# A list scheduler in the source for the S4D half of a two-layer kernel, and x's statistics moved to ScalarE

## The chip, the cores and the metric

One core of a Trainium2 chip runs the whole program. The engines are TensorE (PE in the profile; its weight loads PEld), VectorE (DVE), ScalarE (ACT), GpSimd (POOL) and SyncE (SP), which here only issues DMAs. The metric is the device time of one execution in microseconds (us), median of several runs. Each engine works through its own queue in order; waits between engines go through semaphores.

## The reference

The input x is 2048 x 640, one batch. Everything is float32.

```python
mod = (_silu(c) @ w_mod).reshape(c.shape[0], 6, 1, -1)
sa, ca, ga, sb, cb, gb = (mod[:, 0], mod[:, 1], mod[:, 2], mod[:, 3], mod[:, 4], mod[:, 5])
h = _layernorm(x, axis=-1) * (1 + ca) + sa
x = x + ga * _A_ref(h, ...)
h = _layernorm(x, axis=-1) * (1 + cb) + sb
x = x + gb * _B_ref(h, B_w1, B_w3, B_w2)
```

_A_ref is an S4D convolution along the 2048 positions: for each of the 640 channels the filter is K[l] = 2 Re sum over n of C[n] exp(A[n] dt l), with 128 complex modes n, and y = irfft(rfft(h, 4096) rfft(K, 4096)) + h D_skip. _B_ref is a gated FFN, (silu(h w1) * (h w3)) w2, with 1728 hidden units.

## The kernel before

The convolution is done by hand-written Fourier stages on TensorE, in five blocks of 128 channels (NB = 5). A block needs these pieces, named by the tiles that the profile shows:

- **Filter generation**, eight chunks of 16 channels (gen_chunk). POOL adds phases from two small tables (p to ph) and multiplies magnitudes from two tables of exponentials e (to yy and xx); ScalarE takes two sines and an absolute value per chunk (sn, ph, cs); DVE multiplies (five instructions, to yy and xx); TensorE forms 64 small products (kps), and ScalarE copies two chunks at a time out (ks). The tables p come from five integer shifts on DVE (tile step) and additions on POOL; the tables e from 24 small exponentials of al on ScalarE (param_exp).
- **h**, four pieces of 512 positions: x's columns are loaded again (xq), two rounds of four scalar_tensor_tensor on DVE apply the layer norm and the modulation rows rw (h_make, to xq and hb), a DMA stores hb to DRAM (hs), and one fetch brings the block's h back in another layout (xb).
- **The first stage**, 8 items from xb and 8 from ks, all into PSUM tiles ps, evicted to sp.
- **The spectra**, 8 steps: fh (from h) is copied to hz by ScalarE, two fk (from the filter) are multiplied with hz on DVE (fp), fz is the inverse step on TensorE, evicted to zt and stored to DRAM (zd).

The parameters of block 0 are worked out at the very start (param_part, some 30 DVE instructions over 128x128), those of blocks 1 to 4 together in batch (L798, the same over 128x512, tiles e and scratch). The start-up (early, L807) also loads x once in full (xs) for the layer norm's statistics (bn_stats on DVE, h_st), and w_mod, whose first half gives the rows rw (pm, prow) and whose second half gives the columns cols by three mod_col. The table wb of the spectra uses the memory that parts of w_mod and log_A held, so its load comes after them.

The order: every instruction up to the last spectra goes through the wrappers InOrder (L80 to 90), which chain each engine's instructions in the order of the source; that is why nearly all of them have line L88 in the profile, and groups are told apart by tile. After the start-up comes block 0's first stage, then batch, then the spectra of block 0 with the generation and the h of block 1 merged in by hand-set fractions of the TensorE work (merge L934, beside L947), then for each block its first stage and spectra with the next block's generation and h, and last the fifth block with the first two FFN weight splits (wh, wl) and some inverse rows (iy). Three PSUM banks (tag f) serve ps, fh, fk and fz.

After that the scheduling framework orders the rest: the remaining inverse rows (iy), the second layer norm and transposes (tp, ln2), and the FFN (gu, acc), in four blocks of 512 positions.

Of the kernel before, what the change touches and what calls it, by code (L numbers as in the profile page):

```python
# [10 lines left out]
F32 = mybir.dt.float32  # L11
# [18 lines left out]
EXPS = [(0, 0, i, 64 * i) for i in range(1, 8)] + [(1, 0, k, 512 * k) for k in range(1, 4)] + \  # L30
       [(0, 1, i, i) for i in range(1, 8)] + [(1, 1, k, 32 + 8 * k) for k in range(4)] + [(1, 2, k, 8 * k) for k in range(1, 4)]
# [66 lines left out]

class K:
# [34 lines left out]
    def rsqrt(self, pool, mv, n, tag):  # L134

        nc = self.nc
        v = pool.tile([P, n], F32, name=f"rs_v_{tag}", tag="rs_v")
        yi = pool.tile([P, n], I32, name=f"rs_y_{tag}", tag="rs_y")
        t = pool.tile([P, n], F32, name=f"rs_t_{tag}", tag="rs_t")
        nb = pool.tile([P, n], F32, name=f"rs_n_{tag}", tag="rs_n")  # L140
        nc.vector.tensor_scalar(v, mv[:, :, 1], EPS, None, op0=ALU.add)
        nc.vector.tensor_scalar(yi, v.bitcast(I32), 1, None, op0=ALU.logical_shift_right)
        nc.vector.tensor_scalar(yi, yi, -1.0, float(0x5F3759DF), op0=ALU.mult, op1=ALU.add)
        y = yi.bitcast(F32)
        for _ in range(3):
            nc.vector.tensor_mul(t, y, y)
            nc.vector.scalar_tensor_tensor(t, t, -0.5, v, op0=ALU.mult, op1=ALU.mult)
            nc.vector.scalar_tensor_tensor(y, t, 1.5, y, op0=ALU.add, op1=ALU.mult)
        self.last_rs = nc.vector.scalar_tensor_tensor(nb, mv[:, :, 0], -1.0, y, op0=ALU.mult, op1=ALU.mult)
        return y, nb  # L150
# [9 lines left out]
    def ln_end(self, pool, st, mv, tag):  # L160
        for j in range(4):
            self.nc.vector.bn_aggr(mv[:, j, :], st[:, j, :, :])
        return self.rsqrt(pool, mv, 4, tag)
# [17 lines left out]
    def mod_load_rows(self, k):  # L181
        self.nc.sync.dma_start(self.wm[k], self.w_mod[k * P:(k + 1) * P, :3 * D])

    def mod_row(self, pm, k):

        w = self.wm[k]
# [4 lines left out]

    def mod_rows(self, pm, ps):

        nc = self.nc
        m = self.ring("m")
        nc.gpsimd.memset(m[96:, 384:], 0.0)
        nc.scalar.activation(m[:, :384], pm[:, :384], AF.Copy)
        nc.scalar.activation(m[:96, 384:], pm[:96, 384:], AF.Copy)
        rows = self.rows
        for g in range(4):  # L200
            n = 512 if g < 3 else 384
            pr = ps.tile([P, 512], F32, name=f"prow{g}", tag="f", bufs=self.fb)
            nc.tensor.matmul(pr[:, :n], bc(self.ident[:, 32 * g], 1, P), m[:, :n], start=True, stop=True)
            for a in range(3):
                lo, hi = max(g * 512, a * D), min(g * 512 + n, a * D + D)
                if lo < hi:
                    nc.scalar.activation(rows[a][:, lo - a * D:hi - a * D], pr[:, lo - g * 512:hi - g * 512], AF.Copy)
        self.rA, self.rB = rows[1], rows[0]

    def mod_scale(self):  # L210
        nc = self.nc
        nc.vector.scalar_tensor_tensor(self.rA, self.rA, 1.0, self.rows[2], op0=ALU.add, op1=ALU.mult)
        nc.vector.tensor_mul(self.rB, self.rB, self.rows[2])

    def mod_load(self, a, w):
        self.nc.sync.dma_start(w, self.w_mod[:, (3 + a) * D:(4 + a) * D].rearrange("(k p) d -> p k d", p=P))

    def mod_col(self, ps, a, w):

        nc = self.nc  # L220
        m = self.ring(f"mc{a}")
        pm = ps.tile([P, 512], F32, name=f"pm{a}", tag="f", bufs=self.fb)
        for k in range(KT):
            for g in range(3):
                n = 256 if g < 2 else 128
                nc.tensor.matmul(pm[g * 32:(g + 1) * 32, :n], bc(self.sc[:, k], 1, 32), w[:, k, g * 256:g * 256 + n],
                                 start=(k == 0), stop=(k == KT - 1), tile_position=(0, g * 32))
        nc.scalar.activation(m[:96, :128], pm[:96, :128], AF.Copy)
        nc.scalar.activation(m[:64, 128:256], pm[:64, 128:256], AF.Copy)
        pv = pm[:, 256:262]  # L230
        nc.tensor.matmul(pv[:, 0:5:2], m[:96, :128], self.ident[:96, 0:96:32], start=True, stop=True)
        nc.tensor.matmul(pv[:, 1:4:2], m[:64, 128:256], self.ident[:64, 0:64:32], start=True, stop=True)
        add, mul = ((0.0, 1.0), (1.0, 1.0), (0.0, 0.5))[a]
        nc.vector.tensor_scalar(self.cols[:, a, :], pv[:, :KT], add, mul, op0=ALU.add, op1=ALU.mult)
# [10 lines left out]
    def h_stats(self, e, xs, b):  # L245
        nc = self.nc
        st = e.tile([P, 4, 2, 6], F32, name=f"h_st{b}", tag="h_st", bufs=2)
        for j in range(4):
            for h in range(2):
                nc.vector.bn_stats(st[:, j, h, :], xs[:, j, h * 320:(h + 1) * 320])  # L250
        for j in range(4):
            nc.vector.bn_aggr(self.h_mv[:, b * 4 + j, :], st[:, j, :, :])

    def h_scale(self):
        nm = self.gp.tile([P, NJ], F32, name="h_nm")
        self.nc.vector.tensor_scalar(nm, self.h_mv[:, :, 0], -1.0, None, op0=ALU.mult)
        self.h_rs = self.rsqrt(self.gp, self.h_mv, NJ, "h")[0], nm

    def h_load(self, pool, pc, b):
        t = pool.tile([P, 4, P], F32, name=f"xq{pc}{b}", tag="xq", bufs=2)  # L260
        self.x_slots(t, b, pc * P, pc * P + P)
        self.xq[pc, b] = t
# [85 lines left out]
    def param_alpha(self, ps, tag, bufs, bs):  # L348
        la = self.la[:, bs]
        n = la.shape[1]  # L350
        self.nc.vector.tensor_mul(la, la, bc(self.dts[0][:, bs], 2, P))
        pt = self.turn(ps, tag, bufs, la)
        self.nc.scalar.activation(self.al[:, bs], pt, AF.Copy)

    def param_exp(self, b, sl=slice(None)):

        E = self.E[b % 2]
        for t, m, i, k in EXPS[sl]:
            self.nc.scalar.activation(E[t][:, :, m, i], self.al[:, b], AF.Exp, scale=-float(k))

    def param_mag(self, b):
        V = self.nc.vector
        e2 = self.E[b % 2][1][:, :, 0]
        V.tensor_copy(e2[:, :, 0], self.mag[:, b])
        V.tensor_mul(e2[:, :, 1:4], e2[:, :, 1:4], bc(self.mag[:, b], 2, 3))

    def param_part(self, T, bs, mid=(None, None)):

        V, A = self.nc.vector, self.nc.scalar
        dtb, dt2b = (bc(x[:, bs], 2, P) for x in self.dts)  # L370
        cr, ci, ai, ar, aim, mx, m, k, at, s, fi = (T[x] for x in self.PARTS)


# [748 lines left out]
```

## Time and profile before

| | us |
|---|---|
| median of 3 runs | 1152.91 (1150.5 to 1154.26) |
| the profiled execution | 1157.82 |
| its span, first to last instruction | 1156.0 |
| TensorE busy | 983.8 (85% of the span) |
| TensorE weight loads busy | 800.1 (69%) |
| VectorE busy | 694.3 (60%) |
| ScalarE busy | 481.1 (42%) |
| GpSimd busy | 250.9 (22%), none of note after the last block's generation |
| mean granted TensorE clock | 0.934 |

The tables below the page's first part give busy time by stretches of the span. Rows of groups read: line, engine, operation, output<-inputs, shapes, count, then busy us and mean ns of one, then the idle time of the engine before them and what ended it. Rows of a timeline read: start, length, engine, line, operation, count, and in brackets the idle time before. A row of the chain of waits reads: start, length, what.

### The profile page before, as it was taken

How to read it: one execution, taken by the hardware profiler on the slowest of the kernel's cores; microseconds unless marked ns; L12 is line 12 of the kernel's file. 1: busy time of each engine (PE TensorE's matmuls, PEld its weight loads, DVE VectorE, ACT ScalarE, POOL GpSimd, SP SyncE). 2: the span in 40 equal slices, each digit the busy share in tenths (PEclk: the TensorE clock that was granted, in tenths of full speed). 3: DMA queues.
4: the chain of work that ended last, by engine and by line, in shares of the span. 5: the costliest groups of instructions: out<-in, count | busy, mean ns of one | idle time of the engine just before them, and what ended most of it. 6: DMA issues, size and time to landing. Idle time of an engine off the chain costs nothing.

```text
span 1156.0 us, 21214 instructions
## 1 busy us (share of the span) xinstructions
PE 983.8 (85%) x8663; PEld 800.1 (69%) x8663; DVE 694.3 (60%) x1263; ACT 481.1 (42%) x766; POOL 250.9 (22%) x226
## 2 busy tenths in 40 slices
PE   1445537887978979995999999999999999999996
PEld 0222526675876868974776888888888888888885
DVE  7872389879799697353676654545445454454432
ACT  5341445756657546431432433434334333333322
POOL 5750066565664746000000000000000000000000
PEclk9766867898998989997899999999999999999998
DMA  9829002322322413756874333523335333353311
GB/s 208 217 48 303 5 1 74 75 56 56 84 50 63 103 47 93 184 137 165 230 175 115 103 91 89 150 82 101 92 91 149 85 102 87 92 151 88 92 46 46
DMA packets 142978, 122.11 MB, mean 106 GB/s; under 512 B 14112, under 2 KB 125472, under 8 KB 141344
## 3 DMA queue, kind: packets, MB, share of 16 engines
q1 hardware_dynamic: 142880, 120.75, 39.8%
q8 instruction: 68, 1.11, 0.4%
q14 instruction: 30, 0.25, 0.1%
HBM read 99.75 MB, written 20.97 MB: 104 GB/s over the span
## 4 chain that ended last, share of the span: by engine, by line
PE 69%; DVE 14%; DMA 7%; ACT 4%; issue 3%; SPq 1%; POOL 1%; DVEq 0%; ACTq 0%
PE gu L738 11%; PE gu L739 11%; PE gu L740 11%; PE fz L88 6%; PE acc L773 5%; PE acc L774 5%; PE acc L775 5%; PE fk L88 4%; PE ps L88 3%; DVE yy L88 3%; DVE xq L88 2%; DVE hb L88 2%; PE kps L88 2%; DMA xs<-in_x 2%; PE fh L88 2%
## 5 line engine op out<-in xcount | busy, mean ns | idle before, releaser
L739 PE MATMUL gu<-xl,wh 128*128 128x512 f32 x540 | 212.3, 393 | 0.0
L738 PE MATMUL gu<-xh,wh 128*128 128x512 f32 x540 | 211.7, 393 | 0.5 <-ACT xh L668 0.5
L740 PE MATMUL gu<-xh,wl 128*128 128x512 f32 x540 | 211.4, 392 | 0.0
L88 PE MATMUL fz<-fp,wz 128*128 128x256 f32 x320 | 91.4, 429 | 46.3 <-DVE fp L88 46.0
L643 ACT ACTIVATE wh<-wr 128x640 fp32r<-128x640 f32 x105 | 71.9, 731 | 136.6 <-PE gu L739 131.3
L738 PEld LDWEIGHTS gu<-xh,wh 128*128 128x128 f32 x540 | 101.6, 188 | 25.5 <-issue 1.0
L739 PEld LDWEIGHTS gu<-xl,wh 128*128 128x128 f32 x540 | 101.8, 188 | 21.8
L740 PEld LDWEIGHTS gu<-xh,wl 128*128 128x128 f32 x540 | 101.6, 188 | 21.7
L88 POOL TENSOR_TENSOR yy<-e,e 128x512 f32<-128x512 f32 x80 | 87.4, 1113 | 114.4 <-PE kps L88 73.9
L88 PEld LDWEIGHTS fz<-fp,wz 128*128 128x128 f32 x320 | 63.4, 211 | 61.6 <-DVE fp L88 49.6
L773 PE MATMUL acc<-ah,w2h 128*128 128x512 f32 x260 | 103.8, 399 | 0.0
L774 PE MATMUL acc<-ah,w2l 128*128 128x512 f32 x260 | 102.2, 393 | 0.0
L706 POOL MEMSET w2l<- 64x640 f32 x3 | 1.9, 626 | 450.3 <-PE acc L774 450.3
L775 PE MATMUL acc<-al,w2h 128*128 128x512 f32 x260 | 96.4, 391 | 0.0
L753 DVE SCALAR_TENSOR_TENSOR a<-th,gu 128x512 f32<-128x512 f32 x52 | 35.7, 687 | 99.2 <-ACT th L752 99.0
L754 DVE TENSOR_TENSOR a<-a,gu 128x512 f32<-128x512 f32 x52 | 35.8, 688 | 97.2 <-PE gu L740 97.2
L88 PE MATMUL kps<-yy,xx 128*32 128x64 f32 x2560 | 56.8, 251 | 43.1 <-DVE xx L88 43.1
L88 PEld LDWEIGHTS kps<-yy,xx 128*32 128x32 f32 x2560 | 49.7, 127 | 62.3 <-issue 28.4
L644 DVE TENSOR_TENSOR wl<-wr,wh 128x640 fp32r<-128x640 f32 x105 | 82.2, 818 | 10.8 <-ACT wh L643 10.8
L752 ACT ACTIVATE th<-gu 128x512 f32<-128x512 f32 x52 | 31.1, 598 | 134.7 <-PE gu L740 134.7
L88 PE MATMUL fk<-sp,wb 128*64 128x128 f32 x1280 | 83.8, 281 | 1.9 <-ACT hz L88 1.9
L88 DVE TENSOR_TENSOR fp<-fk,hz 128x512 f32<-128x512 f32 x80 | 53.9, 686 | 47.7 <-PE fk L88 43.0
(190 smaller groups left out, 1711.6 us busy)
## 6 DMA issues: line engine op xcount, KB each, us to landing
wr<-in_w SPq DMA_DIRECT2D x104, 320.0 KB, 3.9
w2r<-in_w SPq DMA_DIRECT2D x52, 320.0 KB, 3.0
zd<-zt SPq DMA_DIRECT2D x40, 256.0 KB, 2.3
iz<-zd SPq DMA_DIRECT2D x24, 320.0 KB, 6.4
xs<-in_x SPq DMA_DIRECT2D x16, 320.0 KB, 14.9
xq<-in_x SPq DMA_DIRECT2D x80, 64.0 KB, 2.4
hs<-hb SPq DMA_DIRECT2D x20, 256.0 KB, 2.4
xb<-hs SPq DMA_DIRECT2D x20, 256.0 KB, 4.9
```

What stands on the lines that cost most here:

```text
L88: self.prev = self.k.order(f(*a, **kw), self.prev)
L643: self.nc.scalar.activation(H, v, AF.Copy)
L644: eng.tensor_tensor(Lo, v, H.bitcast(F32), op=ALU.subtract)
L738: nc.tensor.matmul(pg, wh[:, i, k, :], xh[:, k, :], start=(k == 0), stop=False)
L739: nc.tensor.matmul(pg, wh[:, i, k, :], xl[:, k, :], start=False, stop=False)
L740: nc.tensor.matmul(pg, wl[:, i, k, :], xh[:, k, :], start=False, stop=(k == KT - 1))
L752: nc.scalar.activation(th, gu[0], AF.Tanh, scale=0.5)
L753: nc.vector.scalar_tensor_tensor(a, th, 1.0, gu[0], op0=ALU.add, op1=ALU.mult)
L754: nc.vector.tensor_mul(a, a, gu[1])
L773: nc.tensor.matmul(acc[k], w2h[:, sl], ah, start=(m == 0), stop=False)
L774: nc.tensor.matmul(acc[k], w2l[:, sl], ah, start=False, stop=False)
L775: nc.tensor.matmul(acc[k], w2h[:, sl], al, start=False, stop=(m == 12))
```

## The change

A class Plan holds tasks: name, engine (or a choice of two), duration as written in the source, the tasks needed before, buffers taken and given back, a rank, whether it uses the port that POOL and DVE share, and bytes of DMAs. Its run method places the tasks one at a time, each on the engine where it can start first by these durations, the rank deciding among those that could start within 0.25 us, and calls the function that emits its instructions. So the order of the instructions on each engine still is fixed by the source, through the same wrappers; only what decides it is new. The functions batch, early, beside, merge, stages, gen_block, spectra and first_stage become task lists. Cut to its core:

```diff
-EXPS = [(0, 0, i, 64 * i) for i in range(1, 8)] + [(1, 0, k, 512 * k) for k in range(1, 4)] + \
-       [(0, 1, i, i) for i in range(1, 8)] + [(1, 1, k, 32 + 8 * k) for k in range(4)] + [(1, 2, k, 8 * k) for k in range(1, 4)]
+EXPS = ((0, 0, 0, 64.0), (0, 1, 0, 1.0), (1, 0, 0, 512.0), (1, 1, 4, 8.0), (1, 2, 0, 8.0))
...
+class Plan:
+    LAG = dict(PE=0.2, DVE=0.1, ACT=0.1, POOL=0.1, SP=0.0)
...
+                        if t[5] and s < port:
+                            s = port
...
+                m = min(c)[0]
+                x = min((y for y in c if y[0] <= m + near), key=lambda y: (y[1], y[0]))
...
+            if f:
+                f(e) if isinstance(eng, tuple) else f()
...
-    def h_stats(self, e, xs, b):
-                nc.vector.bn_stats(st[:, j, h, :], xs[:, j, h * 320:(h + 1) * 320])
-            nc.vector.bn_aggr(self.h_mv[:, b * 4 + j, :], st[:, j, :, :])
+        def sums(j):
+            nc.scalar.activation(xs[:, j], xs[:, j], AF.Copy, accum_out=self.h_nm[:, 4 * b + j:4 * b + j + 1])
+        def mean():
+            o = slice(4 * b, 4 * b + 4)
+            nc.vector.tensor_scalar(self.h_nm[:, o], self.h_nm[:, o], -1.0 / D, None, op0=ALU.mult)
+        def squares(j):
+            s = slice(4 * b + j, 4 * b + j + 1)
+            nc.scalar.activation(xs[:, j], xs[:, j], AF.Square, bias=self.h_nm[:, s], accum_out=self.h_ss[:, s])
...
+    def h_norm(self, pc, b):
+        for j in range(4):
+            s = slice(4 * b + j, 4 * b + j + 1)
+            self.nc.scalar.activation(x[:, j], x[:, j], AF.Identity, scale=rstd[:, s], bias=nb[:, s])
+    def h_mul(self, pc, b, eng):
+        eng.tensor_tensor(x, x, bc(self.rA[:, pc * P:pc * P + P], 1, 4), op=ALU.mult)
+    def h_add(self, pc, b, eng):
+        eng.tensor_tensor(hb, x.rearrange("p j (i a) -> p a j i", a=4),
+                          bc(self.rB[:, pc * P:pc * P + P].rearrange("p (i a) -> p a i", a=4), 2, 4), op=ALU.add)
...
-            for dst, src, k in ((p1[:, :, :, 0], by_t(pB), 0), (st[:, 0], pS, 1), (st[:, 1], pS, 2),
-                                (p2[:, :, :, 1], by_t(pS), 3), (p2[:, :, :, 2], by_t(pS), 4)):
-                self.last_step = V.tensor_scalar(dst, src, k, None, op0=ALU.logical_shift_left)
+        return [(.45, lambda: add(st[:, 0], pS, pS)),
+                (.45, lambda: add(st[:, 1], st[:, 0], st[:, 0])),
+                (.45, lambda: G.tensor_copy(p1[:, :, :, 0], by_t(pB))),
...
+    def exp_tasks(self, b):
+            self.eng(e).tensor_tensor(x[0], bc(self.al[:, b], 2, 8), bc(self.j8, 1, P), op=ALU.mult)
+        def exps():
+            for t, m, k, s in EXPS:
+                n = 8 if t == 0 else 4
+                A.activation(E[t][:, :, m, :], x[0][:, :, k:k + n], AF.Exp, scale=-s)
+        add(f"mag{b}", ("POOL", "DVE"), (1.08, .68), lambda e: self.eng(e).tensor_tensor(E[1][:, :, 0], E[1][:, :, 0], bc(self.mag[:, b], 2, 4), op=ALU.mult),
+            [f"exp{b}", f"turn{min(b, 1)}"], t, port=True)
...
+    def pbank(self, name):
+        self.banks += 1
+        if self.banks % 3 == 2:
+            return self.psx.tile([P, 512], F32, name=name, tag="x")
+        return self.psg.tile([P, 512], F32, name=name, tag="f", bufs=2)
...
+            add(n + "f", "PE", .92, lambda i=i: of_h(i), first, t, take=[("bank", 1)])
+            add(n + "h", "ACT", .6, lambda i=i: hold(i), [n + "f"], t - q, take=[("hz", 2)], give=[("bank", n + "f")])
+            add(n + "z", "PE", 1.76, lambda i=i: inverse(i), [n + "x0", n + "x1"], t + W["late"], take=[("bank", 1)],
...
+        for k in range(KT):
+            add(f"c{k}", "SP", 0, lambda k=k: load_w(k), ["x3", "h0.3.l"] + ([f"c{k - 1}"] if k else []), W["col"] + k, dma=[983040], take=[("xs", 1)])
...
+        S = lambda b: 80.0 + 62 * b
```

Beside the order, these pieces of work differ:

- x's statistics: instead of 32 bn_stats and 16 bn_aggr on DVE, 32 passes over 128x640 on ScalarE (16 sums, 16 sums of squared deviations) and four small DVE instructions.
- h: instead of 8 DVE instructions over 128x128 per piece, 4 ScalarE instructions over 128x128 (h_norm) and a multiply and an addition over 128x512 on DVE or POOL (in block 0 on DVE).
- The tables p: POOL makes the shifted copies by additions, for all but the first table.
- The tables e: one product of al with 0 to 7 over 128x1024 (al8, on POOL or DVE) and five exponentials of 1024 or 512 elements on ScalarE, in place of 24 of 128; mag is one multiply in place of a copy and a multiply.
- w_mod's second half comes as five row pieces (c0 to c4) that share the buffers of xs, and one set of products gives all cols.
- The parameters of blocks 1 to 4 (some 29 instructions, seven of which may go to POOL by choice) are tasks with a rank early in the start-up; D_skip is added to ks in four pieces.
- fz and first-stage evictions may go to ScalarE or DVE.

On SP the new order in the start-up is: parameters of all blocks, x's first two pieces, w_mod's first half around x's third, the small tables, x's fourth, block 0's four xq, then c0, wb, c1, c2, the first store of h, c3, two stores, c4, the last store, and the fetch of xb.

1052 lines of the change are left out of this document (609 added, 443 removed).

## The prediction

> **What bounds the kernel now.** I read first the busy time of each engine by stage, cut where the work changes, then the chain that ended last, then the groups and the timeline of one stage. Columns of the first view: stretch in us, its length, busy time of TensorE, of its weight loads, of VectorE (DVE), ScalarE (ACT) and GpSimd (POOL) with counts, granted clock, DMA share, GB/s.
>
> ```profile
> 0.00:40.00 40.00, 12.61 (x161) 5.75 (x161) 33.06 (x104) 20.87 (x47) 25.18 (x34) 1.00 0.95 240
> ...
> 0.00:116.31 116.31, 45.21 (x673) 25.60 (x673) 75.62 (x204) 44.53 (x80) 52.85 (x56) 0.77 0.72 193
> 116.31:131.54 15.23, 15.20 (x257) 14.96 (x256) 0.17 (x1) 8.98 (x15) 0.00 (x0) 1.00 0.03 8
> 131.54:153.47 21.93, 4.76 (x22) 4.30 (x23) 19.83 (x32) 6.49 (x15) 2.00 (x2) 0.61 0.00 0
> 153.47:192.00 38.53, 18.48 (x269) 15.18 (x268) 32.68 (x47) 18.42 (x35) 30.35 (x28) 0.76 0.14 37
> 271.00:350.00 79.00, 67.46 (x1153) 58.16 (x1153) 66.40 (x111) 48.46 (x78) 47.50 (x40) 0.95 0.27 69
> 472.97:531.30 58.33, 58.20 (x656) 49.42 (x656) 23.10 (x46) 19.86 (x33) 0.63 (x1) 1.00 0.68 176
> 565.00:1156.00 591.00, 581.55 (x2634) 469.56 (x2632) 297.33 (x515) 205.72 (x317) 1.88 (x3) 0.99 0.39 103
> ```
>
> From 565 on TensorE is busy 581.55 of 591 us; the change doesn't touch that part. Before it lie 531.3 us in which TensorE is full only at the end (472.97 to 531.30, 58.20 of 58.33, the last block's first stage and spectra). The start-up takes 116 us, then 15 us of first stage, then 22 us in which DVE works out the parameters of blocks 1 to 4 (the "batch") while TensorE has 4.76 us of work, then a slow stretch, then periods of 79 us for each block. The chain of waits (start, length, what) gives the prices of TensorE's work at full clock and what the start-up waits for:
>
> ```profile
> 29.32 16.83 DMA xs<-in_x
> 101.20 14.06 DMA wb<-in_t_wb
> 300.92 1.10 PE kps L88 x61
> 472.97 15.31 PE ps L88 x254
> 503.79 1.87 PE iy L88 x8
> 510.59 1.87 PE iy L88 x8
> ```
>
> One block's first stage is 15.3 us. The last block's spectra are 58.33 - 15.31 - 2 x 1.87 = 39.3. A chunk's product kps is 1.10, eight are 8.8. So a block costs TensorE 15.3 + 39.3 + 8.8 = 63.4 us, and a period takes 79.0: 15.6 us are lost. Timeline rows show most of them (start, length, engine, what, idle before):
>
> ```profile
> 349.84 3.78 PE L88 MATMUL fz<-fp,wz 128*128 128x256 f32 x8 [6.89 <-DVE fp L88]
> ...
> 299.03 1.89 PE L88 MATMUL fz<-fp,wz 128*128 128x256 f32 x8
> ...
> 257.06 4.78 DVE L88 SCALAR_TENSOR_TENSOR xq<-xq,h_nm,rw 128x128 f32<-128x128 f32 x4
> 261.76 5.23 DVE L88 SCALAR_TENSOR_TENSOR hb<-xq,rs_y_h,rw 128x128 f32<-128x128 f32 x4
> ...
> 271.63 1.13 DVE L88 SCALAR_TENSOR_TENSOR xq<-xq,h_nm,rw 128x128 f32<-128x128 f32 x4
> 272.68 1.50 DVE L88 SCALAR_TENSOR_TENSOR hb<-xq,rs_y_h,rw 128x128 f32<-128x128 f32 x4
> ...
> 259.50 2.19 POOL L88 TENSOR_TENSOR yy<-e,e 128x512 f32<-128x512 f32 x2
> ...
> 279.79 1.95 POOL L88 TENSOR_TENSOR ph<-p,p 128x1024 int32<-128x1024 int32 x1
> 294.32 2.09 POOL L88 TENSOR_TENSOR yy<-e,e 128x512 f32<-128x512 f32 x2 [1.96 <-PE kps L88]
> ```
>
> At the block boundary TensorE waits 6.89 us for DVE's product fp, and the matmuls after the wait run at half pace (3.78 against 1.89 us). DVE was late because eight instructions of h (xq, hb) took 4.78 + 5.23 = 10.0 us while POOL was working, against 1.13 + 1.50 = 2.6 while it was not. POOL's own pair took 2.19 instead of 2.09.
>
> **The change, part by part.** The sum is made on the end of the last spectra: Ts (block 0's spectra start), plus four periods, plus the last spectra with their two iy (39.3 + 3.7 = 43.0). Afterwards the instruction order is the same as before (iy, tp, gu), and the weights of the first two FFN steps are still split beside the last spectra, so 531.3 to the end moves as it is. The numbers count instructions in the new order of each engine.
>
> *Ts: batch, statistics and loads.* The batch goes from 131.54-153.47 into the start-up, so it leaves a stretch where nothing covered it. bn_stats leave DVE; 32 ScalarE passes over 128x640 come in (sum, then squares). No row has a ScalarE pass with an accumulator; the nearest is a plain 128x640 pass.
>
> ```profile
> L643 ACT ACTIVATE wh<-wr 128x640 fp32r<-128x640 f32 x105 | 71.9, 731 | 136.6 <-PE gu L739 131.3
> L88 DVE BATCH_NORM_STATS2 h_st<-xs 128x6 f32<-128x320 f32 x32 | 12.9, 475 | 4.6 <-DMA wz<-in_t_wz 4.6
> L88 DVE SCALAR_TENSOR_TENSOR hb<-xq,rs_y_h,rw 128x128 f32<-128x128 f32 x16 | 6.1, 445 | 0.0
> L88 DVE SCALAR_TENSOR_TENSOR xq<-xq,h_nm,rw 128x128 f32<-128x128 f32 x16 | 4.5, 348 | 0.0
> ...
> L88 ACT ACTIVATE al<-ptp 128x128 f32<-128x128 f32 x1 | 0.3, 277 | 2.5 <-PE ptp L88 2.5
> L88 DVE TENSOR_TENSOR fp<-fk,hz 128x512 f32<-128x512 f32 x18 | 12.1, 685 | 6.1 <-PE fk L88 5.9
> ```
>
> ScalarE: 44.5 + 32 x 0.73 (23.4; between 23 and, at double, 47) + 16 normalisations x 0.28 (4.5) + eight of the first stage's evictions x 0.6 (4.8) = 77 us, below 100 even with its waits for x's loads, which now hold the sines queued behind them. DMA: 193 GB/s x 116.3 us = 22.4 MB, at the 240 GB/s of the first 40 us 93 us; the loads are the same, but the table wb no longer stands at the end (101.20, 14 us). On SP the store of the last h piece and the fetch of xb now stand behind the last piece of w_mod's second half, which waits until TensorE has read an earlier piece; while TensorE is that idle in the start-up (45.2 of 116.3) this stays inside DMA's 93. DVE: 75.6 - 12.9 (statistics) - 10.6 (xq, hb) + 19.8 (batch) + 8 x 0.69 (5.5, the h multiplies and adds, now 128x512) + some 2.6 small = 80 us. But some 33 of these (25 of the batch, eight of h) have their operands in SBUF and run beside POOL now. The rows give 0 (POOL idle) to (10.0 - 2.6) / 8 = 0.9 us more for each, so 0 to 30 us; I take 0.6 each, 20, since POOL will have few gaps there. DVE then is done near 100 and is what ends last; the last chunk's product, its eviction and two first-stage items add 4. **Ts = 104**, ends 96 (no such waits, DMA's 93 and the fetch) and 124 (all waits plus what they pass on to POOL).
>
> *A period.* POOL now does 47.5 + ten copies and additions of 128x128 that replace DVE's shifts (5.0) + al8 (2.0, as ph) + mag (1.1) + about four of the eight h multiplies and adds (4.4) = 60 us. These rows price them:
>
> ```profile
> L88 POOL TENSOR_TENSOR p<-p 128x128 int32<-128x128 int32 x2 | 1.0, 500 | 0.0
> L88 POOL TENSOR_TENSOR xx<-e,e 128x512 f32<-128x512 f32 x8 | 8.9, 1112 | 0.0
> L88 POOL TENSOR_TENSOR ph<-p,p 128x1024 int32<-128x1024 int32 x8 | 15.7, 1962 | 3.3 <-ACT cs L88 3.2
> ...
> L88 DVE SCALAR_TENSOR_TENSOR hb<-xq,rs_y_h,rw 128x128 f32<-128x128 f32 x16 | 9.9, 680 | 0.0
> L88 DVE SCALAR_TENSOR_TENSOR xq<-xq,h_nm,rw 128x128 f32<-128x128 f32 x16 | 8.8, 607 | 0.0
> ...
> L88 ACT ACTIVATE sn<-ph 128x1024 f32<-128x1024 int32 x8 | 8.2, 1027 | 6.0 <-DVE xx L88 6.0
> L88 ACT ACTIVATE e<-al 128x128 f32<-128x128 f32 x24 | 6.1, 438 | 0.0
> L88 ACT ACTIVATE hz<-fh 128x512 f32<-128x512 f32 x8 | 4.8, 595 | 5.6 <-PE fh L88 5.6
> ```
>
> DVE loses 18.7 (xq, hb of a period), gains some four h instructions (2.8, and 3.6 of waits), so 66.4 falls to about 54. ScalarE: 24 small exponentials (6.1) become two of 1024 and three of 512 elements (3.9, by sn and hz); 16 normalisations add 4.5: 48.5 becomes 51. So TensorE's 63.4 is the longest, POOL's 60 next. The boundary stall (6.9) and the matmuls at half pace behind it (some 2.5) go, because h of the next block is made during the spectra and its store and fetch are queued ahead of need on SP; its xq loads come behind zd stores there, with buffers for two, and are issued a third of a period early. Without both a period would be 79.0 - 9.4 = 69.6. Of the remaining 6.2 of short stalls I let 4 stand: **67.4**, ends 63.4 and 69.6. Two PSUM buffers and one instead of three in one pool are the same three, and cost nothing unless their order of release differs (0 to 1 us).
>
> Sum: 104 + 4 x 67.4 + 43.0 = 416.6 against 531.3: **-114.7**. The profiled execution took 1157.8 us (span 1156.0); it becomes 1043.1. The median of the runs is 1152.9, so 4.9 lower: **1038 us**. Own range: Ts 96 and 63.4 give 392.6, so 1014; Ts 110 and 69.6 give 431.4, so 1053.
>
> **The rivals.** *Period bound by POOL and the port it shares.* For it: POOL's 60 us against 63.4 leave 3.4, and each DVE operation on SBUF may hold POOL 0.1 (2.19 against 2.09) up to 0.69. Against: POOL makes the next block's phases ahead, so its work may spread over the whole period. The page "SBUF — State Buffer" of the Trainium skill, section "Who interferes with whom", says that a VectorE instruction with two SBUF inputs contends with a GpSimd one that reads SBUF, and that the second to issue blocks until the first has finished; the rows agree for DVE (0.9 us each) and show much less for POOL. By that rule POOL's 60 would grow by 0.69 for each of some five such DVE instructions, to 63.4, level with TensorE; by the rows to 60.5. The forecast needs neither. With periods between 72 and today's 79 the end is 435 to 463, the time 1057 to 1085; middle 1071.
>
> *The start-up doesn't shrink.* The batch in a POOL-laden stretch pays the full 30 us and delays the chunks, or ScalarE's waits for x hold the sines: Ts = 124, 20 later, 1058. For it: the 116 us before were full of waits, and one ScalarE queue now carries loads' waits; against: no engine's sum reaches 116.
>
> *Slower.* Each engine runs a fixed order made from durations that its author wrote down; an instruction that is late holds all that stand behind it on its engine, and they hold other engines. The stretch 153.47-192.00 shows such a knot: TensorE busy 18.48 of 38.53 with DVE 32.68 and POOL 30.35. It decides from periods of (531.3 - 104 - 43) / 4 = 96 us on, where TensorE's share falls under 66%; at 100 us the end is 547, +15.7, 1169. Against it: today's periods, also with fixed orders, have 85%.
>
> **How the numbers follow.** First forecast (1014 to 1053) 0.60, POOL-bound periods 0.20, long start-up 0.14, slower 0.05, and 0.01 for an end within 0.3%, which is what this measurement can tell from no change. So faster 0.94, same 0.01, slower 0.05. The range is 1010 to 1082: below the floor of 1014 by the spread of the runs, up to nearly the whole of the two milder rivals.
>
> **What would show it.** Right: the first fk and fz of block 0 near 104 instead of behind 170; no stretch with TensorE idle and DVE alone; fz of successive blocks 67 us apart; no 7 us wait for fp at a boundary; h's DVE instructions near 0.7 to 1.6 us; the last fz near 417; the same 625 us behind it. Wrong: POOL without gaps and kps waiting for it (first rival); sines behind x statistics, or batch operations of 1.5 us and more (second); TensorE under 70% in the periods (third). A different clock or length behind the last spectra would make the prediction wrong in a part that I take as unmoved.

## The result, and the profile after

| | before | after |
|---|---|---|
| median of 4 runs each, same chip, us | 1153.59 (1150.5 to 1156.32) | 1072.07 (1071.69 to 1072.32) |
| ratio after to before | | 0.9294, 95% interval 0.9269 to 0.9318 |
| profiled execution (span), us | 1157.82 (1156.0) | 1072.27 (1070.5) |
| block 0's spectra start (Ts), us | 152.4 | 127.3 (forecast 104) |
| mean of the four periods, us | 84.0 (79.0 from 271 to 350) | 68.6 (forecast 67.4) |
| last spectra and two iy, us | 43.0 | 44.8 (forecast 43.0) |
| behind them, us | 624.7 | 624.0 (forecast unmoved) |

Before, block 0's spectra begin at 152.4 and the last block's at 488.2, by TensorE's timeline:

```profile
152.37 1.53 PE L88 MATMUL fh<-sp,wb 128*128 128x128 f32 x8
...
158.94 1.02 PE L88 MATMUL fz<-fp,wz 128*128 128x256 f32 x4
...
488.21 1.18 PE L88 MATMUL fh<-sp,wb 128*128 128x128 f32 x8
```

The four periods between them take 335.8 us, 84.0 each in the mean. The kernel became 81.5 us faster by the medians, and 1038 was forecast, 34 us less than the 1072.07 measured. Of the 85.5 us by which the span is shorter, Ts gives 25.1 and the four periods 61.4; the last spectra take 1.8 more, the rest 0.7 less. The first view of the changed kernel is busy time by stage, with the columns of the prediction's first view: the start-up, the four periods, the last spectra, the rest.

```profile
0.00:127.27 127.27, 58.23 (x889) 38.72 (x889) 92.17 (x181) 90.66 (x160) 73.11 (x88) 0.83 0.66 177
127.27:401.74 274.47, 260.09 (x4611) 228.17 (x4609) 202.21 (x289) 203.97 (x293) 222.65 (x203) 0.99 0.36 92
401.74:446.50 44.76, 42.74 (x400) 34.07 (x400) 20.20 (x41) 12.57 (x21) 0.00 (x0) 1.00 0.51 133
446.50:1070.50 624.00, 600.32 (x2712) 485.08 (x2712) 312.09 (x553) 215.48 (x329) 4.45 (x5) 0.98 0.42 110
```

Four periods take 274.47, so 68.6 each, with TensorE busy 260.09 of it; here the change did nearly what was forecast. In the start-up no engine is busy for more than 92 of 127 us. The timeline of TensorE at its end (start, length, engine, line, operation, and in brackets the idle time before and its releaser):

```profile
114.39 1.96 PE L87 MATMUL kps<-yy,xx 128*32 128x64 f32 x64 [2.72 <-DVE xx L87]
116.28 9.28 PE L87 MATMUL ps<-wk,xb 128*64 128x128 f32 x128
125.38 1.96 PE L87 MATMUL ps<-wk,ks 128*64 128x128 f32 x32
127.27 1.18 PE L87 MATMUL fh<-sp,wb 128*128 128x128 f32 x8
```

The group of all fz (count, busy us, mean ns, then the idle time before them):

```profile
L87 PE MATMUL fz<-fp,wz 128*128 128x256 f32 x320 | 79.3, 391 | 1.0 <-DVE fp L87 1.0
```

The last chunk's kps comes at 114.4, then all eight items of h's first stage and the last two of the filter's, and the first fh 12.9 us behind it. And in the periods the wait for fp at a block boundary (6.89 us before) is gone: all 320 fz together were waited for 1.0 us.

What came first in the start-up is in the timelines of ScalarE, POOL and DVE:

```profile
23.64 1.95 POOL L87 TENSOR_TENSOR ph<-p,p 128x1024 int32<-128x1024 int32 x1
...
23.55 0.74 ACT L87 ACTIVATE xs<-xs 128x640 f32<-128x640 f32 x1 [3.49 <-DMA xs<-in_x]
...
37.53 0.81 ACT L87 ACTIVATE xs<-xs,h_nm 128x640 f32<-128x640 f32 x1
39.74 1.03 ACT L87 ACTIVATE sn<-ph 128x1024 f32<-128x1024 int32 x1
...
40.88 0.69 DVE L87 SCALAR_TENSOR_TENSOR yy<-yy,sn 128x512 f32<-128x512 f32 x1 [5.29 <-ACT sn L87]
```

Chunk 0's phases were ready at 25.6 (23.64 + 1.95). Its sine ran at 39.74, because ScalarE's fixed order has seventeen statistics passes ahead of it, with a wait of 3.49 us for a piece of x among them. DVE stood idle for that sine for 5.29 us; what this is worth at the end of the start-up is measured in experiment 1.

### The profile page after: what moved, and what is told of

It reads as the page before. It is cut to its first block, busy times and chain, and to the rows that moved or that the text cites. A ratio compares the mean times of both kernels' runs of the same rounds, so it can differ in the third digit from the quotient of the medians.

```text
span 1070.5 us, 21066 instructions
## 1 busy us (share of the span) xinstructions
PE 961.4 (90%) x8609; PEld 786.0 (73%) x8609; DVE 626.7 (59%) x1063; ACT 522.7 (49%) x803; POOL 300.2 (28%) x295
## 4 chain that ended last, share of the span: by engine, by line
PE 64%; DVE 1%; ACT 1%; DMA 1%; issue 0%; SPq 0%; ACTq 0%; DVEq 0%
PE gu L658 12%; PE gu L657 12%; PE gu L659 12%; PE acc L692 6%; PE acc L693 6%; PE acc L694 6%; PE fz L87 2%; PE fk L87 2%; PE ps L87 1%; PE iy L551 1%; PE fh L87 1%; PE tp L584 1%; PE to L708 1%; PE kps L87 1%; PE acc L698 0%; PE acc L697 0%
## 5 line engine op out<-in xcount | busy, mean ns | idle before, releaser
L87 POOL TENSOR_TENSOR yy<-e,e 128x512 f32<-128x512 f32 x80 | 84.9, 1083 | 42.1 <-PE kps L87 22.4
L87 PEld LDWEIGHTS fk<-sp,wb 128*64 128x64 f32 x1280 | 71.5, 135 | 17.1 <-issue 9.5
L87 POOL TENSOR_TENSOR ph<-p,p 128x1024 int32<-128x1024 int32 x40 | 80.0, 2000 | 11.2 <-ACT cs L87 10.8
L87 PE MATMUL fz<-fp,wz 128*128 128x256 f32 x320 | 79.3, 391 | 1.0 <-DVE fp L87 1.0
L562 ACT ACTIVATE w2h<-w2r 128x640 fp32r<-128x640 f32 x51 | 37.6, 737 | 81.5 <-issue 42.6
```

The source lines that it names most:

```text
L87: self.prev = self.k.order(f(*a, **kw), self.prev)
L562: self.nc.scalar.activation(H, v, AF.Copy)
```

## The experiments

All kernels but the seventh keep the schedule's order and move, leave out or give to another engine named tasks alone, so that nothing else is ordered anew. The functions that emit a task are collected, moved and then called:

```diff
-            if f:
-                f(e) if isinstance(eng, tuple) else f()
+            if f:
+                calls.append((n, lambda f=f, a=(e,) if isinstance(eng, tuple) else (): f(*a)))
...
+        for names, behind in MOVES:
+            moved = [c for x in names.split() for c in calls if c[0] == x]
+            calls = [c for c in calls if c not in moved]
+            i = [c[0] for c in calls].index(behind) + 1
+            calls[i:i] = moved
+        for _, f in calls:
+            f()
```

Task names: su and sq are a sum and a square pass (piece, row); g0.c.s, .m and .p are chunk c's sines, DVE products and kps in block 0; p1.n are the batch's steps, p1.g POOL's two additions in it, p1.t its transposes; c0 to c4 are the row pieces of w_mod's second half. Ts is read from one profile each; the first kps of the six kernels with edit 1's order up to there lies between 38.5 and 40.3 us, so a difference of Ts below some 2 us says little by itself.

| kernel | Ts, us | median, us | ratio to before (95%) |
|---|---|---|---|
| the changed kernel | 127.3 | 1072.07 | 0.9294 (0.9269 to 0.9318) |
| 1 sines ahead of passes | 122.4 | 1069.75 | 0.9245 (0.9198 to 0.9292) |
| 2 batch out of the way | 132.6 | 1080.82 | 0.9338 (0.9291 to 0.9386) |
| 3 both | 129.1 | 1076.77 | 0.9304 (0.9249 to 0.9359) |
| 4 no statistics | 115.7 | 1062.88 | 0.9184 (0.9139 to 0.9230) |
| 5 as 1, end of start-up | 120.3 | 1066.68 | 0.9230 (0.9203 to 0.9258) |
| 6 as 1, batch again | 129.3 | 1077.76 | 0.9326 (0.9289 to 0.9363) |
| 7 statistics on DVE | 131.2 | 1071.36 | 0.9275 (0.9245 to 0.9305) |
| 8 h on DVE in periods | 127.3 | 1086.19 | 0.9397 (0.9366 to 0.9428) |
| 9 no batch | 118.2 | 1063.27 | 0.9203 (0.9171 to 0.9235) |
| 10 neither | 110.9 | 1056.99 | 0.9149 (0.9113 to 0.9185) |
| 11 as 5, passes in gaps | 119.3 | 1066.43 | 0.9234 (0.9200 to 0.9268) |
| 12 as 11, h's additions on POOL | 120.4 | 1066.14 | 0.9220 (0.9194 to 0.9246) |

### 1. The sines ahead of the statistics

```diff
+MOVES = (
+    ("sq00 sq01 sq02 sq03 su12 su13", "g0.0.s2"),
+    ("mean1", "g0.0.m4"),
+    ("sq10 sq11 sq12 sq13 su20", "p1.8"),
+    ("su21 su22", "g0.2.s2"))
```

> The changed kernel with ScalarE's order alone altered: the sines of chunk 0 stand ahead of ten statistics passes, those of chunk 1 ahead of eight, all other orders as they were (one small DVE instruction follows its passes). Theory A (ScalarE's queue: passes over x ahead of the sines start a chain that is late from there on): first kps near 38 instead of 45.0 us, block 0's spectra 5 to 8 us earlier than 127.3, total 1064 to 1068 instead of 1072. Theory B (the batch and POOL's two batch additions in the middle of generation set the chain): first kps earlier, but the spectra within 2 us of 127.3 and the total 1070 to 1073. Theory C (the path of x's last piece: load, statistics, h, store, fetch): the same as B. The prediction's own logic (the busiest engine's sum): no change, DVE does the same work.

The timelines of ScalarE and TensorE:

```profile
30.47 1.03 ACT L87 ACTIVATE sn<-ph 128x1024 f32<-128x1024 int32 x1
...
38.52 1.09 PE L87 MATMUL kps<-yy,xx 128*32 128x64 f32 x62
109.55 1.96 PE L87 MATMUL kps<-yy,xx 128*32 128x64 f32 x64 [2.72 <-DVE xx L87]
122.41 1.18 PE L87 MATMUL fh<-sp,wb 128*128 128x128 f32 x8
```

The first sine moves from 39.7 to 30.5, the first kps from 45.0 to 38.5, and the last kps and the spectra keep 4.9 us of it. All eleven passes that stood between the first exponentials and the first sine now come behind it. ScalarE's order is a cause, worth about a fifth of the missing 23 us; theory A had expected 5 to 8 us. In the time the gain is not shown: the median is 2.3 us lower, and the ratio to the kernel before, which ran beside it on another chip than in the first comparison, 0.5% lower, but the two intervals overlap.

### 2, 3 and 6. The batch out of generation's way

```diff
+    ("p1.g1 p1.g2", "g0.4.z2"),
+    ("g0.2.m1 g0.2.m2 g0.2.m3 g0.2.m4", "g0.2.m0"),
+    ("p1.23 p1.24 p1.25 p1.26 p1.27 p1.28 p1.t0 p1.t1 g0.1.d", "g0.2.m4"),
+    ("g0.3.s2", "g0.3.s1"),
+    ("su23 su30 su31 su32 su33", "g0.3.s2"))
```

> The changed kernel with two orders altered: POOL's two additions of the batch stand behind chunk 4's magnitudes instead of ahead of chunk 3's, and DVE does chunk 2's products ahead of the batch's last six steps; chunk 3's sines stand ahead of five statistics passes. Theory A: spectra of block 0 within 2 us of 127.3, total 1070 to 1073. Theory B: third kps at 62 to 65 instead of 71.5, the following ones 6 to 10 us earlier too, spectra at 118 to 122, total 1063 to 1067. Theory C: kps earlier as in B, but the fetch of h stays near 107 and the spectra near 125 to 127, total 1070 to 1073.

> Both edits together. If A and B are knots one behind the other on one chain, their gains add: spectra at 112 to 117, total 1058 to 1062. If one of them is the whole cause, this is no better than that one alone. Theory C: the products of generation are done 10 us and more earlier, but the spectra stay at 122 to 127, total 1067 to 1073.

Neither gained: Ts is 132.6 and 129.1, against 127.3 in the changed kernel and 122.4 in kernel 1. The third kps came later instead of earlier, at 77.74 in the first and 74.32 in the second, since TensorE's own order still had the batch's transposes ahead of it. So the third try (6) moves g0.1.d and the third kps, g0.2.p, ahead as well, on top of edit 1.

> The order with the sines ahead, and the batch moved out of generation's way once more, now on every queue: chunk 2's products on DVE and its kps on TensorE stand ahead of the batch's last six steps and transposes, POOL's two additions of the batch behind chunk 4's magnitudes. In the earlier try the third kps stood behind the batch's transposes in TensorE's order and ran at 74.3 with its products done near 61. Theory B: third kps near 61 to 63, spectra at 114 to 119, total 1061 to 1066. Theory of the shared port (a DVE instruction of the batch that runs while POOL works takes 0.3 to 0.9 us longer; in the changed kernel POOL stood idle beside the batch, in the first try it worked and seven of these took 0.9 to 1.6 us): what the chunks gain, the batch loses, and through it everything that waits for the batch: spectra at 120 to 126, total 1068 to 1074.

It was no faster either. Rows of DVE, POOL and TensorE in the changed kernel first, where POOL stands idle behind the batch, and then in try 6, where it works beside it:

```profile
54.73 0.68 DVE L87 TENSOR_TENSOR e<-e 128x512 f32<-128x512 f32 x1
60.29 0.68 DVE L87 SCALAR_TENSOR_TENSOR xb<-xb,e 128x512 f32<-128x512 f32 x1
64.85 1.38 POOL L87 TENSOR_TENSOR xb<-xb,pB 128x512 int32<-128x512 int32 x1 [10.32 <-DVE xb L87]
```

```profile
49.55 1.55 DVE L87 TENSOR_TENSOR e<-e 128x512 f32<-128x512 f32 x1
63.84 1.55 DVE L87 SCALAR_TENSOR_TENSOR xb<-xb,e 128x512 f32<-128x512 f32 x1
64.80 1.51 POOL L87 TENSOR_TENSOR xx<-e,e 128x512 f32<-128x512 f32 x1
60.19 1.96 PE L87 MATMUL kps<-yy,xx 128*32 128x64 f32 x64 [7.89 <-DVE ks L87]
80.57 0.52 DVE L87 TENSOR_SCALAR rs_v_h<-h_ss 128x16 f32<-128x16 f32 x1 [2.99 <-ACT xs L87]
```

The same two steps take 1.55 instead of 0.68 us when POOL works beside them. The third kps does come early (60.2), but the batch ends later, its transposes and the small mean of x's last pieces behind it on DVE too, and the scale of h begins at 80.6 instead of 73.2 in kernel 1 (77.8 in the changed kernel). POOL's 10.3 us of idling beside the batch, which looked like a knot, had left DVE's steps short. None of these three orders makes the start-up shorter than kernel 1's; what a chunk gains the batch loses. That no better place exists for the batch is not shown. Its price beside a working POOL lies within what the prediction allowed for it.

### 4, 9 and 10. What the two moved pieces of work cost

> All 32 passes over x for the statistics, and the four small DVE instructions that serve them, are left out (mean 0 and variance 1 are put in their place), every order else as in the changed kernel; it bounds what the passes cost. Theory A: first kps near 34, spectra at 112 to 118, total 1057 to 1063. Theory B: first kps near 34, but the spectra at 122 or later, total above 1066. Theory C: hscale is free of x's last piece, h and its fetch come some 10 us earlier; spectra at 115 to 120, and the last kps no earlier than now unless A holds too. The prediction's own logic: DVE's sum falls by under 1 us, no change.

> The batch (parameters of blocks 1 to 4: 27 DVE steps, three ScalarE functions, the transposes and POOL's two additions) is left out of the changed kernel, zeros stand for its results, and every other instruction keeps its place; it bounds what the batch costs in the start-up as the run without statistics does for the passes (11.6 us of 127.3). If DVE's sum sets the end (the prediction's logic): DVE loses some 20 us, spectra near 107. If the batch stands on the chain that ScalarE begins (chunk 2's products wait behind it): third kps near 58 instead of 71.5 and spectra at 112 to 118, total 1057 to 1064. If the chain runs beside it through x's last piece, ScalarE's passes and h: spectra at 120 to 126, total 1065 to 1071.

> Statistics passes and batch both left out, every other instruction at its place: what the start-up takes without the two pieces of work that the change moved there or to ScalarE. If the two cost one behind the other, the spectra start 11.6 us plus the batch's own gain before 127.3, at 98 to 106; if they run side by side and each is the other's cover, the two together gain clearly more than their sum (under 98); if loads and the fetch of h set the end, 110 to 116, not much below 115.7.

The edit is one line in the loop that calls the tasks (for 10 both conditions), with constants written to the results at the start:

```diff
-        for _, f in calls:
-            f()
+        for n, f in calls:
+            if not (n[:2] in ("su", "sq") or n[:4] == "mean"):   # 4
+            if n[:3] != "p1.":                                   # 9
+                f()
```

TensorE at the end of the start-up, without statistics, without the batch, without both:

```profile
115.70 1.18 PE L87 MATMUL fh<-sp,wb 128*128 128x128 f32 x8
```

```profile
118.21 1.18 PE L87 MATMUL fh<-sp,wb 128*128 128x128 f32 x8
```

```profile
98.00 1.96 PE L87 MATMUL kps<-yy,xx 128*32 128x64 f32 x64 [2.72 <-DVE xx L87]
99.89 9.28 PE L87 MATMUL ps<-wk,xb 128*64 128x128 f32 x128
110.89 1.18 PE L87 MATMUL fh<-sp,wb 128*128 128x128 f32 x8
```

The passes cost 11.6 us of Ts, the batch 9.1, both together 16.4: less than the sum of 20.7, so part of one is hidden beside the other. Every DVE step of the batch gone (some 20 us of work) gives 9 and not 20: DVE's sum does not set the end. Two marks on the way came later than expected: the first kps in 4 at 39.3 (34), the third in 9 at 60.5 (58). And with neither, in this order, the start-up still takes 110.9, of which 12.9 us lie between the last kps and the spectra. By its number this is the third case that was expected, but the fetch of h does not set the end there: its last part was issued at 93.5 and landed within 5.1 us, before TensorE came to it at 99.89, while the last kps waited 2.72 us for DVE. So 104 lay below what this order takes even without the added work.

### 5, 11 and 12. The end of the start-up

Edit 5, on top of 1; cols2 are the three small DVE instructions at the end of mod_cols, made a task of their own:

```diff
+    ("c4", "c3"),
+    ("cols2 inv", "g0.7.m4"),
```

> The order with chunk 0's and 1's sines ahead of the statistics (spectra at 122.4 us there), and two more moves at the end of the start-up: the last piece of w_mod's second half is issued right behind the one before it instead of between two stores of h, and the three small DVE instructions that finish cols stand behind chunk 7's products instead of ahead of its third. Theory C (SP's order and the fetch): the fetch of xb is issued near 99.5 instead of 102.3. Theory of DVE's order: last kps near 107 instead of 109.6. If each of them holds the other's gain (the fetch lands some 5 us after its last issue), both moves together give spectra at 119.5 to 120.5, 2 to 3 us less in all, 1066.5 to 1068; if TensorE's first stage behind the last kps is all that counts, the same; if neither matters, 122.4 and 1069.7.

```profile
99.26 1.75 SPq L87 DMA_DIRECT2D xb<-hs  x4
106.57 1.96 PE L87 MATMUL kps<-yy,xx 128*32 128x64 f32 x64 [0.26 <-DVE xx L87]
120.32 1.18 PE L87 MATMUL fh<-sp,wb 128*128 128x128 f32 x8
```

As expected: the fetch is issued at 99.3 (102.3 in kernel 1, 107.2 in the changed one), the last kps no longer waits 2.7 us, and Ts falls by 2.1, hardly more than two profiles differ by; the median falls by 3.1. These are two waits, one on SP and one on DVE, that the prediction had not priced; what each is worth alone was not measured.

Edit 11 puts passes into gaps of ScalarE's queue; 12 lets POOL do three of h's additions behind chunk 7's phases:

```diff
-    ("sq10 sq11 sq12 sq13 su20", "p1.8"),
-    ("su21 su22", "g0.2.s2"),
+    ("su20 su21 su22", "g0.1.s2"),
+    ("sq10 sq11 sq12 sq13", "p1.8"),
+    ("su23", "g0.2.s0"),
+    ("su30", "g0.2.s1"),
+    ("su31 su32 su33", "g0.2.s2"),
+    ("mean2", "p1.28"),
+    ("sq20 sq21", "mean2"),
+    ("mean3", "p1.v1"),
...
+    ("h0.1.a h0.1.o h0.2.a h0.2.o h0.3.a h0.3.o", "g0.7.ph"))   # 12, with these additions on POOL
```

> The order with the sines ahead, the last piece of w_mod earlier and cols' end later (spectra at 120.3, total 1066.7), and ScalarE's passes over x's third and fourth piece moved into gaps of its queue between 41 and 56 us, so that the scale of h is known some 3 us earlier. If ScalarE's passes at 58 to 73 us set the rest of the start-up: spectra at 116.5 to 118, total 1063 to 1065. If chunk 3's and 4's products or TensorE set it: 119.5 to 120.5, total 1066 to 1067.

> The order with all moves so far (spectra at 119.3 us there, total 1066.4), and three additions of h in block 0, 1.81, 1.07 and 1.11 us on DVE beside POOL, done by POOL in the gap of its queue (90 to 96 us) behind chunk 7's phases; the stores follow them. If DVE's queue with the instructions that it does beside POOL (chunk 5's products wait behind two of them, POOL's next magnitudes for that chunk's kps) sets the end of the start-up: sixth kps near 91.5 instead of 94.2, the fetch near 96 instead of 98.3, spectra at 116 to 117.5, total 1063 to 1065. If POOL's own work is then late or the last chunks are bound by ScalarE: 118.5 to 120, total 1066 to 1068.

Edit 11 brought 1.0 us of Ts, within what two profiles differ by, and nothing in the median; the scale of h begins at 71.5 instead of 72.4, not the 3 us earlier that were expected. In 12 POOL's and TensorE's rows say why nothing came of it:

```profile
90.94 6.84 POOL L87 TENSOR_TENSOR hb<-sp,rw 128x512 f32<-128x512 f32 x3
103.37 1.96 PE L87 MATMUL kps<-yy,xx 128*32 128x64 f32 x64 [0.60 <-DVE xx L87]
108.71 9.91 PE L87 MATMUL ps<-wk,xb 128*64 128x128 f32 x128 [3.38 <-DMA xb<-hs]
```

The last kps is 2.1 us earlier than in 11 (105.5), but POOL needs 2.28 us for an addition (6.84 / 3) where 1.1 was expected, the stores and the fetch come later, and TensorE now waits 3.38 us for xb. In the changed kernel and in kernels 1, 5 and 11 the last part of the fetch lands some 0.5 to 2.5 us before TensorE comes to it (last issue plus the longest time to landing): generation and h end within that of each other, so a gain on one alone is soon lost at the other.

Kernels 5, 11 and 12 cannot be told from each other, and all lie 0.5 to 0.8% below the changed kernel: their intervals end at 0.9258, 0.9268 and 0.9246, that of the changed kernel begins at 0.9269. The step is small, and for 11 the intervals all but touch.

### 7. The statistics back on DVE

```diff
+                add(f"su{b}{j}", "DVE", .95, lambda b=b, j=j: st[b][0](j), [f"x{b}"], t + .01 * j, give=[("xs", f"x{b}")])
+            add(f"mean{b}", "DVE", .9, lambda b=b: st[b][1](), [f"su{b}{j}" for j in range(4)], t)
...
+                nc.vector.bn_stats(t[:, j, h, :], xs[:, j, h * 320:(h + 1) * 320])
```

> One part of the change undone: x's statistics on DVE as before (32 bn_stats, 16 bn_aggr and 8 small instructions), the task list and its ranks otherwise as they are; the scheduler orders everything anew. ScalarE loses its 32 passes, some 29 us with their accumulator reads; DVE gains some 16 to 18 us. Theory A (ScalarE's queue): the sines come early, spectra at 114 to 121, total 1060 to 1067. The prediction's own logic (DVE's sum ends last): 13 us and more later, spectra at 138 to 145, total 1083 to 1090. If both engines are about equally in the way: 122 to 132.

Ts is 131.2, at the upper end of the third case, and the time is that of the changed kernel: 1071.36, the intervals nearly the same. In the first 115 us DVE is busy for 100.41 instead of 86.56 and ScalarE for 59.56 instead of 84.41 (busy time by stage, kernel 7 and then the changed kernel):

```profile
0.00:115.00 115.00, 49.18 (x729) 26.88 (x729) 100.41 (x221) 59.56 (x88) 67.47 (x83) 0.80 0.67 188
```

```profile
0.00:115.00 115.00, 45.96 (x689) 26.85 (x693) 86.56 (x171) 84.41 (x153) 65.15 (x81) 0.82 0.72 194
```

In kernel 7 TensorE's timeline ends its start-up with a wait for the fetch of h:

```profile
118.38 10.96 PE L87 MATMUL ps<-wk,xb 128*64 128x128 f32 x128 [3.40 <-DMA xb<-hs]
```

Shifting 13.9 us of DVE's work to 24.8 us of ScalarE's moved Ts by 3.9 and the total by nothing that can be measured. The scheduler ordered everything around it anew, so this compares two whole schedules: with this scheduler it does not matter to the time which engine does the statistics.

### 8. POOL's share of h in the periods given to DVE

```diff
+                if n[0] == "h" and n[-2:] in (".x", ".a"):
+                    e = "DVE"
```

> The changed kernel with the 14 multiplies and additions of h that the schedule gave to POOL in the four periods done by DVE at the same places. POOL loses 15 us over four periods, DVE gains 10. If POOL bounds the periods (the prediction's first rival): periods fall from 68.6 to about 65, total near 1058. If TensorE and its short waits bound them: mean period 68 to 70, total 1070 to 1078, more on the side of slower since DVE's products fp stand behind the additions.

The first period of the changed kernel, then of this one:

```profile
127.27:191.50 64.23, 62.20 (x1123) 54.97 (x1121) 49.76 (x72) 49.58 (x76) 55.78 (x52) 1.00 0.34 85
```

```profile
127.27:199.08 71.81, 63.31 (x1122) 55.96 (x1120) 56.67 (x77) 49.93 (x76) 49.49 (x47) 0.98 0.30 76
```

TensorE's timeline in this kernel has one of the new waits, for a chunk's product that stands behind a multiplication of h on DVE (2.36 us, from 139.85):

```profile
142.96 1.96 PE L87 MATMUL kps<-yy,xx 128*32 128x64 f32 x64 [3.46 <-DVE xx L87]
```

POOL's load falls from 55.78 to 49.49, DVE's rises from 49.76 to 56.67, and the period grows by 7.6 us though neither is busy for more than 57 of 72. The mean period is 72.0 (from 127.27 to 415.23), and the total of 1086 lies above the 1078 expected too: over the four periods POOL loses 21.8 us and DVE gains 15.1, more than the 15 and 10 expected. So POOL's load does not bound the periods, and the first rival falls in that part. In the four periods TensorE waits 9.9 us for xx from DVE in this kernel, 3.3 in the changed one: TensorE plus what stands in front of its operands in DVE's order is what these rows show.

## Why the prediction was right or wrong

The time of 1072 lies inside the range of 1010 to 1082, but above the first forecast's own 1014 to 1053. It lies next to the middle of the first rival, 1071, and that is luck: the rival reaches it by periods of 72 to 79 us, and they took 68.6. What came true is the first forecast in the periods and a start-up as long as the second rival's.

**Right: the periods' length and loads.** Forecast 67.4, measured 68.6 in the mean; the other three by stage:

```profile
191.50:262.00 70.50, 65.21 (x1091) 56.78 (x1089) 47.86 (x70) 51.50 (x76) 56.95 (x55) 0.98 0.33 83
262.00:328.50 66.50, 64.11 (x1155) 56.58 (x1153) 53.09 (x76) 52.65 (x72) 61.84 (x56) 1.00 0.29 75
328.50:401.70 73.20, 68.53 (x1251) 59.80 (x1249) 51.51 (x75) 50.24 (x69) 48.08 (x43) 1.00 0.46 120
```

The loads came as worked out: in the mean of a period POOL 55.7 (222.65 / 4; 60 predicted), DVE 50.6 (54), ScalarE 51.0 (51). The stall of 6.9 us at the boundary went. Small waits, most of them for kps and ks, take some 3.6 us a period (68.6 - 260.09 / 4) where 4 were left; the 1.2 that were short are TensorE's own time, 65.0 instead of 63.4. The periods before were longer than the prediction read: 79.0 is one of them, the mean of the four is 84.0. The sum, which starts from 531.3, does not depend on it, but a period fell by 15.4 us in the mean where 11.6 were forecast. Which part of the change did this, the order, h's new form or the engines that share it, no experiment separates; kernel 8 shows only that the periods get longer when DVE does POOL's share of h. The sign "the first fk and fz of block 0 near 104 instead of behind 170" was misread too: before, the first fk came at 153.8 and the first fz at 158.9.

**Right: what lies behind the last spectra** did not move (624.0 against 624.7).

**A size: the last spectra**, 44.8 instead of 43.0. DVE's additions for two iy and 16 bn_stats of the second layer norm stand between products fp on DVE; TensorE waited 0.98 us for such an addition and 1.00 us for the fp behind them.

```profile
431.65 1.08 PE L87 MATMUL iy<-iz,wd 128*64 128x512 f32 x4 [0.98 <-DVE x L87]
435.75 1.97 PE L87 MATMUL fz<-fp,wz 128*128 128x256 f32 x8 [1.00 <-DVE fp L87]
```

**Wrong: Ts = 104.** It was 127.3, and these 23.3 us are most of the 29 by which the profiled execution missed 1043.1 (the periods gave 4.9, the last spectra 1.8, the rest -0.7; 4.9 more had been taken off because the profiled execution of before was slower than its median, which that of after is not). Two sentences of the prediction failed. The first, "DVE then is done near 100 and is what ends last", takes the end of the start-up as the busiest engine's sum with no idle time on it. DVE's work was even less than was added up: 86.6 us busy by 115 us, against 80 and 20 of waits. But it also stood idle for 28 of these 115, most of it for ScalarE (the longest waits were 6.6 us for block 0's exponentials and 5.3 for chunk 0's sine), and the last kps came at 114.4. Experiment 1 shows one such wait and its worth (4.9), experiment 5 two more (together some 2.1). Experiment 4 takes no more than four small instructions from DVE and gains 11.6, experiment 9 takes some 20 us from it and gains 9.1; 10 shows that the two together cost 16.4 and that what is left needs 110.9 in this order. The second, "two first-stage items add 4", was 12.9: all eight items of h's first stage came behind the last kps. TensorE's order puts them there, and the fetch of xb, issued from 107.2 to 109.7 and up to 6.0 us in landing, would have let them start little earlier. The prediction saw that the fetch stood behind w_mod's last piece and let DMA's 93 us cover it; it did not ask when h would be ready for the store, which waits for the statistics of x's last piece.

**Half seen: the second rival.** "ScalarE's waits for x hold the sines" is close to what experiment 1 shows (the passes themselves hold them longer than the 3.49 us of waiting for x), and its Ts of 124 was near; its other half, the batch at full contended price, is not what happened. As a rival it got 0.14 because no engine's sum reached 116. That again takes an engine's sum for the end of the stage.

**Prices.** The 32 passes took 24.6 us (11.6 and 13.0, a mean of 0.737 and 0.814 each), 23.4 predicted: right, and not what decided: their place in the order did. The 0.6 us of waits for each DVE step beside POOL lies inside what was measured where POOL worked: five steps of try 6 took 1.54 or 1.55 us instead of 0.68, others 0.80 to 1.14. In the changed kernel's batch only two steps paid plainly from 45 us on (2.25 and 1.28 us, at 51.35 and 53.53); then POOL stood idle for 10.3 us. It was paid in h, where two of the steps took 1.81 and 2.44 us and chunk 5's product stood behind them. Not all of the 1.81 is a wait: with POOL idle (96.45 to 102.60) such an addition of h took 1.07 and a multiplication 0.68, where the prediction had 0.69 for both:

```profile
92.83 1.81 DVE L87 TENSOR_TENSOR hb<-sp,rw 128x512 f32<-128x512 f32 x1
94.56 2.44 DVE L87 TENSOR_TENSOR sp<-sp,rw 128x512 f32<-128x512 f32 x1
96.92 0.68 DVE L87 TENSOR_TENSOR xx<-sn,xx 128x512 f32<-128x512 f32 x1
...
98.65 1.07 DVE L87 TENSOR_TENSOR hb<-sp,rw 128x512 f32<-128x512 f32 x1
...
100.24 0.68 DVE L87 TENSOR_TENSOR sp<-sp,rw 128x512 f32<-128x512 f32 x1
```

By the Trainium skill's page "SBUF — State Buffer", section "Who interferes with whom", the second of two such instructions blocks until the first is done: the 1.55 and 2.44 against 0.68 agree with that for DVE. POOL's own rows show less, 1.51 against 1.06 for the same xx beside try 6's batch.

**Still open:** what the shortest start-up of this work would be, why what is left without passes and batch still needs 110.9, and which part of the change shortened the periods. The lowest Ts with all the work done is 119.3 (11).

## What to carry to other kernels

The busiest engine's sum bounds a stage from below; when every engine has gaps, follow the first and the last product of the stage through each queue and add what stands in front of it. Work that is moved to an engine with free time costs by its place in that engine's order: 25 us of passes cost 11.6 us of the end here, eleven of them standing between the first exponentials and the first sines 4.9. Where two chains of work meet (here generation and h), look which of them is late before shortening one, and before freeing an idle engine, ask what it will slow down once it works.

## What the runs showed of the hardware that was not expected

Multiplications and additions of h have the same size, but not the same price on POOL. In the four periods of the changed kernel, the groups by form (count, then busy us, mean ns):

```profile
L87 POOL TENSOR_TENSOR xq<-xq,rw 128x512 f32<-128x512 f32 x11 | 14.1, 1284 | 0.8 <-DMA xq<-in_x 0.8
L87 POOL TENSOR_TENSOR hb<-xq,rw 128x512 f32<-128x512 f32 x4 | 8.6, 2154 | 3.3 <-DVE xq L87 3.2
```

The multiply reads its rows in sequence; the addition reads both inputs with a step of four elements, 16 bytes, and takes 2154 ns. The Trainium skill's page "GPSIMD Engine Reference", section "7. Performance pitfalls for Q7 kernels", gives some half more per element for reads with a step above 8 bytes, in custom kernels; 2154 / 1284 is 1.68, so the direction agrees for this built-in instruction and the size is larger. DVE shows the same direction, 1.07 against 0.68 us. No run changes the step alone, so that it is the cause is argued, not shown. The prediction had 1.1 us for both on POOL.

A pass with an accumulator on ScalarE is followed by an instruction of its own that reads it (ACTIVATION_READ_ACCUMULATOR, 0.19 us), but successive passes start 0.72 us apart (17.80, 18.52 and 19.24 in the changed kernel), the length of the pass: the read is hidden.
